# Attention and top-1 MoE in one kernel: more row blocks transposed by DMA, a filled row ring, more output buffers

## The chip, the cores and the metric

One core of one Trainium2 chip. The metric is the device time of one execution in microseconds, the median of several runs. TensorE (PE, with its weight loads PEld), VectorE (DVE), ScalarE (ACT), GpSimd (POOL) and SyncE (SP) each run their own instructions in order. SP issues most DMAs, POOL the indirect ones (gathers and scatters of rows).

## The reference

A causal attention over a window of 64 positions (8 batches, 8 heads, 576 positions, 64 wide), and behind it a mixture of 8 experts of which each token takes one:

```python
scores = scale * np.matmul(q, k.transpose(0, 1, 3, 2))
mask = (rel >= 0) & (rel < 64)               # rel = query position - key position
attn = softmax(np.where(mask, scores, -1e9))
x = np.matmul(attn, v)                       # as 4608 rows of 512
logits = x @ w_gate                          # 8 experts
e = argmax(logits); gate_w = softmax(logits)[e]
out = gate_w * (relu(x @ w1[e]) @ w2[e])     # w1 512 x 1024, w2 1024 x 512
```

All of it is float32. The kernel splits each operand of the expert matmuls into a high and a low part (names ending in h and l, or hi and lo) and adds three products.

## The kernel before

**Attention.** A loop over 36 tiles of 128 rows (variable i, to 42 because each tile goes through stages) makes scores, exponentials, transposes, values and rows, writes each tile of rows to `xs` in DRAM, and computes its routing. q, k and v come through a ring in SBUF, which is given back after the loop (`st.close()`), so that later pools take its place.

**Early passes.** The routing of the first 16 and 28 tiles gives a fixed list of rows for four experts, e = 0 to 3. Each early pass takes two blocks of 128 rows of one expert: POOL gathers them into `xg`, `turn` (four PE transposes into PSUM, then a copy on ACT and a subtraction on DVE) lays them out by columns, and `expert` runs over 8 slices j of the hidden width. Pass e = 0 starts inside the attention loop (`forward`), the rest follow it in a loop of steps, seven to a slice.

**A slice.** `expert` splits the weights of the next slice (`split_`: ACT makes `whi` from `raw`, L252, DVE makes `wlo`, L249), does eight hidden matmuls with whi (L322) and four with wlo (L326), then `hh` on ACT (L332) and `hl` on DVE (L333). `flush` then does the output matmuls of the slice before (L294), and after the last slice scales each block into a `ys` buffer on ACT (L281), which POOL scatters to `out` (L282). `hw` gives ys three buffers.

**Weights.** A load on SP (L234) brings a piece of 1 MB, two slices; there are three buffers. In an early pass `split_` asks for the piece after next use only when a piece is begun: piece 2 (slices 4 and 5) at the top of slice 1. The first piece of the next pass is asked for after slice 3. Late passes have `far=True`, which asks earlier.

**Plan and late passes.** While the early passes run, `steps` advances once per step: `plan` computes on DVE how the remaining rows are cut into late passes (many small operations), then `parts` makes six large tables (`here` once, `said` five times, 128 x 1152), and `table` (36 matmuls) gives row numbers for the late passes. `get` gathers their rows into `late_rows`, two buffers of four blocks. Since rows beyond the end are not written, POOL clears both buffers by eight memsets (L1002), one per slice step. Late pass 0 (two blocks) is turned by PE (`flip`) in slices 5 and 6 of the last early pass. From late pass 1 on, `chain` lays out the rows of the next pass without PE: `part` copies 16-bit halves to `planes` on DVE (L832) and issues a DMA transpose on SP (L835), `join` puts the halves together on ACT (L839), `lay` makes xh and xl (L847, L848). Eleven late passes are always there; widths run from 256 to 512 rows, four of them with four blocks.

The order on every engine is the order in which the code emits (`manual_schedule`).

Of the kernel before, what the change touches and what calls it, by code (L numbers as in the profile page):

```python
# [129 lines left out]
def window_attention_then_top1_moe(ctx: ExitStack, tc: tile.TileContext, qkv, wall, wg, cst, out):  # L130
# [141 lines left out]
    def flush(final=False):  # L272

        if not late:
            return
        (hh, hl), yp, (hi, lo), j, w, last = late.pop()
        def finish(u):
            n = min(P, w - u * P)
            ix, gate = last[0][u][0:n], last[1][u][0:n]
            ys = hw.tile([P, C], F32, name="ys")  # L280
            nc.scalar.activation(out=ys[0:n], in_=yp[u][0:n], func=AF.Copy, scale=gate)  # L281
            ins = nc.gpsimd.indirect_dma_start(  # L282
                out=out, out_offset=bass.IndirectOffsetOnAxis(ap=ix, axis=0), in_=ys[0:n], in_offset=None,
                bounds_check=N - 1, oob_is_err=False)

            for o in outs:
                tc.declare_no_dep(ins.ins, o.ins, reason="scatters to rows of their own")
            outs.append(ins)

        for u, y in enumerate(yp):  # L290
            n = min(P, w - u * P)
            us = slice(u * P, u * P + n)
            for m, (x, ww) in enumerate(((hh, hi), (hh, lo), (hl, hi))):
                nc.tensor.matmul(y[0:n], lhsT=x[:, us], rhs=ww[:, C:], start=(j == 0 and m == 0),  # L294
                                 stop=(j == NJ - 1 and m == 2))
            if final:
                finish(u)
            if u + 1 < len(yp):
                yield
        if last is not None and not final:  # L300
            for u in range(len(yp)):
                finish(u)
        yield
# [399 lines left out]
    def plan():  # L703
# [93 lines left out]
        keep["want"] = want  # L797
        for b in parts(xn, want[:, 0:NMA], NT, NMA):
            keep["said"] = b
            yield  # L800
            yield

    def table(lo, hi):
        read(gathered(keep["said"], NT, hi - lo, t_b), hi - lo, idx_sb[:, lo:hi], gate_sb[:, lo:hi])
# [22 lines left out]

    halves, joined = {}, {}

    def part(i, u):  # L830
        pl = xq.tile([P, 2, C], U16, name="planes", bufs=3)
        nc.vector.tensor_copy(out=pl, in_=late_rows[i % 2][:, u].bitcast(U16).rearrange("p (f s) -> p s f", s=2))  # L832
        src = pl.rearrange("p s f -> p (s f)")
        halves[i, u] = xq.tile([P, 2 * 4, P], U16, name="halves", bufs=4)
        nc.sync.dma_start_transpose(out=halves[i, u], in_=src)  # L835

    def join(i, u):
        x = joined[i, u] = xq.tile([P, 4, P], F32, name="joined", bufs=3)
        nc.scalar.copy(out=x.rearrange("p k t -> p (k t)").bitcast(U16).rearrange("p (t s) -> p s t", s=2),  # L839
                       in_=halves.pop((i, u)).rearrange("p (s k) t -> p s (k t)", s=2))  # L840

    def lay(i, u):
        if u == 0:
            xt[i] = columns(xw)
        x, us = joined.pop((i, u)), slice(u * P, (u + 1) * P)
        xh, xl = xt[i]
        nc.scalar.copy(out=xh[:, :, us], in_=x)  # L847
        nc.vector.tensor_tensor(out=xl[:, :, us], in0=x, in1=xh[:, :, us], op=ALU.subtract)  # L848

    def open_weights(i):  # L850
        wts[i] = Weights(expert_of(passes[i][0]), far=True)
# [8 lines left out]
    def first_passes():  # L860
        for e in range(EARLY):
            ms = range(2 * e, 2 * e + 2)
            for j in expert(xe[e % 2], cols(eidx, ms), cols(egate, ms), ew[e],
                            lambda: ew[e + 1] if e + 1 < EARLY else wts[0]):
                if e + 1 < EARLY and j == 3:
                    ew[e + 1] = Weights(e + 1)
                if e + 1 < EARLY and j in (4, 5):
                    turn(xg[(e + 1) % 3], j - 4, xe[(e + 1) % 2])
                    if (e, j) == (EARLY - 2, 5):
                        keep["turned"] = True  # L870
                yield e, j

    def do(what):
        if rs_[what]:
            rs_[what], f = None, rs_[what]
            f()
# [18 lines left out]
    with tc.manual_schedule():  # L895
        keep_busy(BUSY[0])
        for i in range(NS + LAST):
            for c in range(FIRST, 2 * NS):

                if c % 2 and i == (c - RING + 1) // 2 + 4:  # L900
                    load(c)
            if i == LOADW:
                ew[0] = Weights(0, len(QUARTERS))
            if i == SPLIT:
                ew[0].prepare(AHEAD, pieces)
            if i == TURN:
                ew[0].first = ew[0].split()

            rs_["step"] = i
            each(exps, i - 1)  # L910
            each(evac, i - 2)
            each(apart, i - 2)
            for _ in range(1 if i < NS else 2):
                if gets and gets[0][0] <= i:
                    gets.popleft()[1]()
            if i == TURN:
                scored[1].close()
                turns["hp"] = single(1)
            while exs:
                exs.popleft()()  # L920
            if i > 5 and settled:
                settled.popleft()()
            if i > TURN:
                split_ahead()
            forward(i, 0)
            do("first")
            each(scores, i)
            each(folded, i)
            each(largest, i)
            if i < len(BUSY) - 1:  # L930
                keep_busy(BUSY[i + 1])
            forward(i, 1)
            each(values, i - 3)
            if slow and slow[0][0]:
                f = slow.popleft()[1]
                if f:
                    f()
            while begin and begin[0][0] <= i:
                begin.popleft()[1]()
            for c in range(FIRST, 2 * NS):  # L940
                if c % 2 == 0 and i == (c - RING) // 2 + 3:
                    load(c)
            if quarters and quarters[0][0] <= i:
                _, o, w = quarters.popleft()
                nc.sync.dma_start(out=o, in_=w)
            if rs_["fast"] and (rs_["fast"][0][0] < i):
                rs_["fast"].popleft()[1]()
            forward(i, 2)
            each(rows_t, i - 4)
            each(cols_t, i - 4)  # L950
            forward(i, 3)
            each(transp, i - 1)
            if i == TURN - 1:
                scored[0].close()
                turns.update(xp=[t_b], yp=single(0))
                for u in range(2):
                    turn(xg[0], u, xe[0], turns["yp"][u])
            do("last")
            each(shares, i - 3)
            do("read")  # L960
            for k in range(RATE[0] if i < NS else 4):
                if slow and not slow[0][0]:
                    slow.popleft()[1]()
            for k in range(RATE[1] if i < NS else 2):
                if puts and not slow:
                    puts.popleft()()
            while lows:
                lows.popleft()()
            if pieces:
                pieces.popleft()()  # L970
# [4 lines left out]
        xw = ctx.enter_context(tc.tile_pool(name="xw", bufs=2))  # L975
        xn = ctx.enter_context(tc.tile_pool(name="xn", bufs=1))
        late_rows = [xn.tile([P, MOST, C], F32, name=f"rows{i}") for i in range(2)]
        clear = deque(t[:, u] for t in late_rows for u in range(MOST))
        xq = ctx.enter_context(tc.tile_pool(name="xq", bufs=2))
        turns["xp"].append(m_b)  # L980
        turns["yp"] = [x_b[:, 0], x_b[:, 1], *turns["yp"]]

# [1 line left out]
        def steps():  # L984
# [3 lines left out]
            for _ in range(WAIT[1]):  # L988
                yield
            table(0, NMA)  # L990
            while "turned" not in keep:
                yield
            get(0)
            yield
            open_weights(0)
            get(1)

        rest = steps()
        for e, j in early:
            next(rest, None)  # L1000
            if clear and j is not None:
                nc.gpsimd.memset(clear.popleft(), 0.0)  # L1002
            if e == EARLY - 1 and j == NJ - 3:
                for _ in rest:
                    pass
            if e == EARLY - 1 and j is not None and j >= NJ - 3:
                flip(0, [j - NJ + 3])

    def chain(first, last):
        for i in range(first, last):  # L1010
# [4 lines left out]
            for j in expert(xt.pop(i), cols(idx_sb, passes[i]), cols(gate_sb, passes[i]), wts.pop(i), fol, widths[i]):  # L1015
                if j is None or i + 1 == last:
                    continue
                if j == 2 and i + 2 < last:
                    get(i + 2)
                if j == 3:  # L1020
                    open_weights(i + 1)
                if j in (4, 6):
                    wts[i + 1].load()
                for u, at in enumerate(JOIN[len(passes[i + 1])]):
                    if j == u // 2:
                        part(i + 1, u)
                    if j == at:
                        join(i + 1, u)
                for u, at in enumerate(JOIN[len(passes[i + 1])]):
                    if j == at + 1:  # L1030
                        lay(i + 1, u)
        for _ in flush(True):
            pass

# [50 lines left out]
```

## Time and profile before

| | |
|---|---|
| three runs, us | 627.82, 628.63 (median), 630.64 |
| profiled execution, own time and span, us | 627.76, 626.0 |
| PE busy | 589.2 (94%) |
| DVE busy | 382.0 (61%) |
| ACT busy | 351.5 (56%) |
| POOL busy | 198.9 (32%) |
| granted TensorE clock, mean | 0.996 of full |
| DMA | 129.17 MB, 206 GB/s on average |

Busy time is that of the engine's own instructions, and the span runs from the first to the last instruction. The rows further below give engine, line, operation, output and inputs by the program's names and, in brackets, idle time before the instruction and what ended it.

### The profile page before, as it was taken

The page shows a single profiled execution, that of the slowest core. Times are in us where ns is not written, and L with a number is a line of the kernel's source. Part 1 is how long each engine was busy: PE and PEld are TensorE (multiplying, and loading weights), DVE is VectorE, ACT ScalarE, POOL GpSimd, SP SyncE. Part 2 cuts the span into 40 slices and gives each one's busy share as a digit, 9 for nine tenths or more (in the row PEclk, how much of TensorE's full clock was granted, in tenths as well). Part 3 has the DMA queues.
Part 4 walks back from the last instruction along what each step waited for, and adds up shares of the span by engine and source line. Part 5 has one row for each costly group of instructions (what it writes and reads, how often), then busy time and mean ns, then how long its engine had stood idle before and what let it go on. Part 6 is the DMA issues. An engine that isn't in the chain of part 4 may idle for free. (4 is left out here: it accounts for less than half of the span.)

```text
span 626.0 us, 15826 instructions
## 1 busy us (share of the span) xinstructions
PE 589.2 (94%) x6491; PEld 504.7 (81%) x6491; DVE 382.0 (61%) x692; ACT 351.5 (56%) x729; POOL 198.9 (32%) x188
## 2 busy tenths in 40 slices
PE   8789988898988999999999999999999899999994
PEld 4678877787777799988888888878878799999983
DVE  3677778996789956658554444345244346667651
ACT  4677766776444536476745446356245445657651
POOL 3656667578242141044040050130220312132011
PEclk9999999999999999999999999999999999999998
DMA  9978888954545476397858275396283454886731
GB/s 311 360 250 293 290 262 287 305 195 159 203 173 177 141 279 238 136 302 186 276 143 289 68 169 222 90 148 256 70 229 130 122 208 109 293 283 189 265 113 36
DMA packets 64387, 129.17 MB, mean 206 GB/s; under 512 B 36268, under 2 KB 37420, under 8 KB 56880
## 3 DMA queue, kind: packets, MB, share of 16 engines
q1 hardware_dynamic: 58000, 109.17, 54.3%
q0 software_dynamic: 6304, 18.88, 9.7%
q8 instruction: 53, 0.87, 0.6%
q14 instruction: 30, 0.25, 0.1%
HBM read 102.34 MB, written 19.53 MB: 195 GB/s over the span
## 5 line engine op out<-in xcount | busy, mean ns | idle before, releaser
L249 DVE TENSOR_TENSOR wlo<-raw,whi 128x1024 fp32r<-128x1024 f32 (+1 forms) x126 | 149.1, 1184 | 77.9 <-ACT whi L252 77.7
L332 ACT ACTIVATE hh<-e_b 128x256 fp32r<-128x256 f32 (+4 forms) x120 | 53.5, 446 | 172.2 <-PE e_b L326 172.0
L282 POOL DMA_INDIRECT out<-ys,idx_sb x32 | 37.0, 1157 | 273.8 <-ACT ys L281 269.2
L252 ACT CAST whi<-raw 128x1024 fp32r<-128x1024 f32 (+1 forms) x121 | 121.4, 1004 | 1.8 <-DMA raw<-wall 1.7
L322 PE MATMUL e_b<-xh,whi 128*128 128x256 f32 (+4 forms) x352 | 109.7, 328 | 3.2 <-ACT whi L252 3.2
L333 DVE SCALAR_TENSOR_TENSOR hl<-e_b,hh 128x256 fp32r<-128x256 f32 (+4 forms) x120 | 59.6, 497 | 85.9 <-ACT hh L332 85.6
L322 PE MATMUL e_b<-xl,whi 128*128 128x256 f32 (+4 forms) x352 | 108.8, 325 | 0.0
L459 POOL TENSOR_TENSOR pm<-tsb,cs 128x512 f32<-128x512 f32 x72 | 90.4, 1277 | 50.5 <-ACT tsb L452 43.1
L322 PEld LDWEIGHTS e_b<-xh,whi 128*128 128x128 f32 x352 | 66.2, 188 | 13.1 <-ACT whi L252 5.4
L326 PE MATMUL e_b<-xh,wlo 128*128 128x256 f32 (+4 forms) x352 | 72.0, 327 | 0.0
L322 PEld LDWEIGHTS e_b<-xl,whi 128*128 128x128 f32 x352 | 66.2, 188 | 6.2
L443 ACT ACTIVATE pf<-s_b,mxs 128x64 f32<-128x64 f32 x288 | 63.1, 339 | 10.5 <-DVE mxs L435 8.6
L473 PE MATMUL x_b<-ring,pm 64*64 64x65 f32 x2176 | 47.8, 222 | 15.4 <-issue 6.5
L326 PEld LDWEIGHTS e_b<-xh,wlo 128*128 128x128 f32 x352 | 56.7, 188 | 4.2 <-DVE wlo L249 0.2
L473 PEld LDWEIGHTS x_b<-ring,pm 64*64 64x64 f32 x2176 | 42.0, 134 | 21.2 <-issue 13.3
L294 PE MATMUL e_b<-whi,hl 128*128 128x512 f32 x144 | 56.4, 392 | 1.0 <-DVE hl L333 1.0
L294 PE MATMUL e_b<-whi,hh 128*128 128x512 f32 x144 | 56.8, 395 | 0.0
L294 PE MATMUL e_b<-wlo,hh 128*128 128x512 f32 x144 | 56.5, 393 | 0.0
L497 ACT COPY xT<-m_b 128x512 f32<-128x512 f32 x36 | 21.1, 587 | 40.9 <-PE m_b L490 40.9
L190 POOL DMA_INDIRECT rows<-xs,idx_sb x32 | 38.4, 1200 | 13.9 <-issue 12.7
L416 PE MATMUL s_b<-ring 64*64 64x128 f32 x1024 | 41.0, 278 | 0.0
L839 ACT COPY joined<-halves 128x1024 uint16<-128x1024 uint16 x30 | 39.9, 1350 | 0.0
(193 smaller groups left out, 1021.3 us busy)
## 6 DMA issues: line engine op xcount, KB each, us to landing
raw<-wall SPq DMA_DIRECT2D x58, 1024.0 KB, 6.1
ring<-qkv SPq DMA_DIRECT2D x66, 386.0 KB, 5.0
xs<-xrow SPq DMA_DIRECT2D x36, 256.0 KB, 3.4
raw<-wall SPq DMA_DIRECT2D x8, 256.0 KB, 5.5
ring<-qkv SPq DMA_DIRECT2D x4, 256.0 KB, 4.6
ring<-qkv SPq DMA_DIRECT2D x4, 130.0 KB, 4.7
ring<-qkv SPq DMA_DIRECT2D x1, 512.0 KB, 3.7
rows<-xs,idx_sb POOLq DMA_INDIRECT x32, 6.4
```

The lines of the kernel that those rows point to most:

```text
L249: nc.vector.tensor_tensor(out=lo[:, s], in0=raw[:, s], in1=hi[:, s], op=ALU.subtract)
L252: nc.scalar.copy(out=hi[:, s], in_=raw[:, s])
L294: nc.tensor.matmul(y[0:n], lhsT=x[:, us], rhs=ww[:, C:], start=(j == 0 and m == 0), stop=(j == NJ - 1 and m == 2))
L322: nc.tensor.matmul(hp[:, 0:w], lhsT=hi[:, ks], rhs=x[:, kk, 0:w], start=(kk == 0 and x is xh), stop=False)
L326: nc.tensor.matmul(hp[:, 0:w], lhsT=lo[:, kk * P:(kk + 1) * P], rhs=xh[:, kk, 0:w], start=False, stop=(kk == 3))
L332: nc.scalar.activation(out=hh[:, 0:w], in_=hp[:, 0:w], func=AF.Relu)
L333: nc.vector.scalar_tensor_tensor(out=hl[:, 0:w], in0=hp[:, 0:w], scalar=0.0, in1=hh[:, 0:w], op0=ALU.max, op1=ALU.subtract)
L416: nc.tensor.matmul(sp[cols, a, g], lhsT=q_r[rows, r, g], rhs=k_r[rows, r - 1:r + 1, g], start=True, stop=True)
L443: nc.scalar.activation(out=pf[:, g, a], in_=sp[:, a, g, 0], func=AF.Exp, bias=mx[:, h:h + 1], scale=SCALE)
L459: nc.gpsimd.tensor_tensor(out=pm[i], in0=t.rearrange("p (g q) -> p g q", g=NG), op=ALU.mult, in1=cc("mask")[:, i * P:(i + 1) * P].unsqueez ...
L473: nc.tensor.matmul(x_b[cols, a, g * V1:(g + 1) * V1], lhsT=pm[i][rows, g, cols], rhs=v_r[rows, c % RING - i, g], start=(i == 0), stop=(i = ...
L839: nc.scalar.copy(out=x.rearrange("p k t -> p (k t)").bitcast(U16).rearrange("p (t s) -> p s t", s=2), in_=halves.pop((i, u)).rearrange("p ...
```

## The change

- `part`, `join` and `lay` take rows and a key instead of a pass, and `prepare` calls them for any pass. Early passes e = 2 and e = 3 are prepared that way during the pass before (slices 0, 4, 5 and 6), and late pass 0 during e = 3 by `ready`. Pass e = 1 is still turned by PE.
- `ready` also holds what `chain` did at slices 3, 4 and 6: it opens the next late pass's weights and loads two pieces. For late pass 0 this now happens in e = 3.
- `get(0)` no longer waits for the last `turn`; `rest` is run to its end after e = 2.
- The late rows are filled by two loads of 1 MB from `xs` on SP instead of by eight memsets on POOL.
- `ys` has five buffers.
- The six parts of the late table are twice as many steps apart, so that the table comes 24 steps later.
- In the last turn of the attention loop the delayed low halves (`lows`) are emitted before the routing work, not after it.

```diff
-            ys = hw.tile([P, C], F32, name="ys")
+            ys = hw.tile([P, C], F32, name="ys", bufs=5)
...
             keep["said"] = b
-            yield
-            yield
+            for _ in range(4):
+                yield
...
+    def part(rows, key):
+        pl = keep["xq"].tile([P, 2, C], U16, name="planes", bufs=3)
+        nc.vector.tensor_copy(out=pl, in_=rows.bitcast(U16).rearrange("p (f s) -> p s f", s=2))
+        halves[key] = keep["xq"].tile([P, 2 * 4, P], U16, name="halves", bufs=4)
+        nc.sync.dma_start_transpose(out=halves[key], in_=pl.rearrange("p s f -> p (s f)"))
...
+    def prepare(j, rows, nu, key, xt):
+        for u in range(nu):
+            at = JOIN[nu][u]
+            if j == u // 2:
+                part(rows[:, u], (key, u))
+            if j == at:
+                join((key, u))
+        for u in range(nu):
+            if j == JOIN[nu][u] + 1:
+                lay((key, u), u, xt())
+
+    def ready(i, j):
...
+        prepare(j, late_rows[i % 2], len(passes[i]), i, columns_of)
+        if j == 3:
+            open_weights(i)
+        if j in (4, 6):
+            wts[i].load()
...
-                if e + 1 < EARLY and j in (4, 5):
-                    turn(xg[(e + 1) % 3], j - 4, xe[(e + 1) % 2])
-                    if (e, j) == (EARLY - 2, 5):
-                        keep["turned"] = True
+                if e == 0 and j in (4, 5):
+                    turn(xg[1], j - 4, xe[1])
+                if 0 < e < EARLY - 1 and j is not None:
+                    prepare(j, xg[(e + 1) % 3], 2, ("early", e), lambda: xe[(e + 1) % 2])
+                if e == EARLY - 1 and j is not None:
+                    ready(0, j)
...
+            if i == NS + LAST - 1:
+                while lows:
+                    lows.popleft()()
...
-        clear = deque(t[:, u] for t in late_rows for u in range(MOST))
-        xq = ctx.enter_context(tc.tile_pool(name="xq", bufs=2))
+        for t in late_rows:
+            nc.sync.dma_start(out=t, in_=xs[0:MOST * P].rearrange("(u p) c -> p u c", p=P))
+        keep["xq"] = ctx.enter_context(tc.tile_pool(name="xq", bufs=2))
...
             table(0, NMA)
-            while "turned" not in keep:
-                yield
             get(0)
             yield
-            open_weights(0)
             get(1)
...
-            if clear and j is not None:
-                nc.gpsimd.memset(clear.popleft(), 0.0)
-            if e == EARLY - 1 and j == NJ - 3:
+            if (e, j) == (EARLY - 2, NJ - 1):
                 for _ in rest:
                     pass
-            if e == EARLY - 1 and j is not None and j >= NJ - 3:
-                flip(0, [j - NJ + 3])
...
-                if j == 3:
-                    open_weights(i + 1)
-                if j in (4, 6):
-                    wts[i + 1].load()
...
+                ready(i + 1, j)
```

## Rows read from the trace of the kernel before

**Rows 1.** Stretches: length, busy time of each engine, granted clock, DMA share, GB/s.

```profile
core 0: us, PE busy (x) PEld busy (x) DVE busy (x) ACT busy (x) POOL busy (x), PEclk, DMA share, GB/s
...
190.00:200.00 10.00, 7.92 (x51) 6.65 (x50) 9.44 (x32) 2.97 (x6) 2.33 (x5) 1.00 0.67 238
210.00:220.00 10.00, 9.09 (x55) 7.40 (x54) 10.00 (x12) 5.13 (x8) 3.19 (x2) 1.00 0.48 158
...
540.00:550.00 10.00, 10.00 (x67) 9.09 (x66) 7.11 (x9) 7.31 (x11) 0.00 (x0) 1.00 0.66 249
```

**Rows 2.** Waits of PE, 176 to 218: total us, times, longest.

```profile
PE e_b L326 <- DVE wlo L249: 2.3, 4, 1.3
PE x_b L294 <- DVE hl L333: 2.0, 2, 1.6
PE e_b L294 <- DVE hl L333: 1.0, 1, 1.0
PE m_b L793 <- DVE xel L204: 0.5, 1, 0.5
```

**Rows 3.** Waits of PE, 355 to 505.

```profile
PE e_b L322 <- ACT whi L252: 3.0, 4, 1.8
```

**Rows 4.** Waits of ACT, 355 to 505.

```profile
ACT ys L281 <- DMA out<-ys,idx_sb: 16.5, 4, 4.3
```

**Rows 5.** Timeline of PE at a turn: start, us, instruction.

```profile
229.66 0.60 PE L201 MATMUL m_b<-cs,xg 128*128 128x128 f32 x4
230.02 0.36 PE L322 MATMUL e_b<-xeh,whi 128*128 128x256 f32 x1
```

**Rows 6.** Timeline of DVE in a late pass of 256.

```profile
550.46 1.28 DVE L832 COPY planes<-rows 128x1024 uint16<-128x1024 uint16 x2
```

**Rows 7.** Timeline of ACT in late pass 0.

```profile
278.72 1.05 ACT L252 CAST whi<-raw 128x1024 fp32r<-128x1024 f32 x1 [1.21 <-DMA raw<-wall]
...
279.94 1.35 ACT L839 COPY joined<-halves 128x1024 uint16<-128x1024 uint16 x1
```

**Rows 8.** Timeline of POOL, the memsets.

```profile
181.13 1.47 POOL L1002 MEMSET rows<- 128x512 f32 x3
...
189.92 2.41 POOL L1002 MEMSET rows<- 128x512 f32 x5
```

**Rows 9.** Timeline of DVE, three small operations of the plan.

```profile
180.38 2.25 DVE L681 TENSOR_SCALAR nbr<-nb 128x8 f32<-128x8 f32 x1
...
183.08 0.16 DVE L681 TENSOR_SCALAR half<-left 128x8 f32<-128x8 f32 x1
...
190.82 1.54 DVE L679 TENSOR_SCALAR l<-l 128x8 f32<-128x8 f32 x1
```

**Rows 10.** Line 234, loads at 196.18 (early), 554.07 and 530.68 (behind transposes).

```profile
DMA to landing us min/median/max: 4.8/4.8/4.8
...
DMA to landing us min/median/max: 6.8/6.8/6.8
...
DMA to landing us min/median/max: 8.1/8.1/8.1
```

**Rows 11.** Timeline of PE, first matmuls of slices 0 and 1 of e = 1.

```profile
184.25 0.28 PE L322 MATMUL e_b<-xeh,whi 128*128 128x256 f32 x1
...
187.06 0.28 PE L322 MATMUL e_b<-xeh,whi 128*128 128x256 f32 x1
```

**Rows 12.** Timeline of PE, the table of the late passes.

```profile
220.79 2.67 PE L640 MATMUL t_b<-said,hot_row 128*128 128x160 bf16 x36
```

**Rows 13.** Timeline of POOL, the first gather of late rows.

```profile
224.69 1.44 POOL L190 DMA_INDIRECT rows<-xs,idx_sb  x1 [4.45 <-issue]
```

**Rows 14.** Line 190, the five gathers of late rows from 224.69 to 230.7.

```profile
DMA to landing us min/median/max: 3.8/5.3/6.7
```

**Rows 15.** Timeline of PE, first matmul of a late pass of 256.

```profile
548.06 0.28 PE L322 MATMUL e_b<-xh,whi 128*128 128x256 f32 x1
```

**Rows 16.** Timeline of SP in the same pass.

```profile
551.17 2.64 SPq L835 DMA_TRANSPOSE halves<-planes  x2
554.07 1.22 SPq L234 DMA_DIRECT2D raw<-wall  x1
```

More of the change, by code (lines that the diff above doesn't have):

```diff
@@ L828, in window_attention_then_top1_moe @@
     halves, joined = {}, {}
[L830 to L838, printed above, removed]
-        nc.scalar.copy(out=x.rearrange("p k t -> p (k t)").bitcast(U16).rearrange("p (t s) -> p s t", s=2),
-                       in_=halves.pop((i, u)).rearrange("p (s k) t -> p s (k t)", s=2))
@@ L842, in lay @@
[L842 to L846, printed above, removed]
+    def part(rows, key):
[3 more added lines that the diff above has]
+        nc.sync.dma_start_transpose(out=halves[key], in_=pl.rearrange("p s f -> p (s f)"))
@@ L847, in lay, with join @@
+    def join(key):
+        x = joined[key] = keep["xq"].tile([P, 4, P], F32, name="joined", bufs=3)
+        nc.scalar.copy(out=x.rearrange("p k t -> p (k t)").bitcast(U16).rearrange("p (t s) -> p s t", s=2),
+                       in_=halves.pop(key).rearrange("p (s k) t -> p s (k t)", s=2))
+    def lay(key, u, xt):
+        x, us = joined.pop(key), slice(u * P, (u + 1) * P)
+        xh, xl = xt
         nc.scalar.copy(out=xh[:, :, us], in_=x)
         nc.vector.tensor_tensor(out=xl[:, :, us], in0=x, in1=xh[:, :, us], op=ALU.subtract)
+    def prepare(j, rows, nu, key, xt):
[8 more added lines that the diff above has]
+                lay((key, u), u, xt())
@@ L850, in open_weights, with columns_of @@
+    def ready(i, j):
+        def columns_of():
+            if i not in xt:
+                xt[i] = columns(xw)
+            return xt[i]
+        prepare(j, late_rows[i % 2], len(passes[i]), i, columns_of)
[3 more added lines that the diff above has]
+            wts[i].load()
     def open_weights(i):
@@ L1019, in chain @@
                     get(i + 2)
-                if j == 3:
-                    open_weights(i + 1)
-                if j in (4, 6):
-                    wts[i + 1].load()
[L1024 to L1031, printed above, removed]
+                ready(i + 1, j)
         for _ in flush(True):
```

## The prediction

> **What bounds the kernel now.** I read a table of stretches first, then what PE waited for, then what ScalarE waited for. In the late passes PE has no gap (10.00 of 10 us in 540 to 550), but in the early ones it has (7.92 and 9.09) while VectorE is at 9.4 to 10 tenths [rows 1]. From 176 to 218 PE waits for VectorE 8 times, 5.8 us in all: for low halves of weights (wlo) and of hidden values (hl), and once for an xel [rows 2]. From 355 to 505 it waits 4 times for whi, 3.0 us [rows 3], and ScalarE, which makes whi, waits as often for a scatter that still reads a ys buffer, 16.5 us [rows 4]. The reader is to see that time can come from these 8.8 us, or from work taken off PE, and from nothing else that the change touches.
>
> Durations come from the profiled execution: span 626.0, its own time 627.76, so 1.76 around. The median shown is 628.63, 0.87 above it. A measurement of this kernel can tell about 0.5% (3.1 us) from no change.
>
> **Part 1, transposes off PE.** Six blocks (two each of early passes e = 2 and e = 3 and of late pass 0) lose their four PE transposes. Such a four begins at 229.66, the next matmul at 230.02 [rows 5]: 6 x 0.36 = 2.1 us less. In their place come, per block, a planes copy on DVE (1.28 for two [rows 6]), a DMA transpose and a joined copy on ACT (1.35 [rows 7]); the copy and the subtraction behind them stay. ACT's 6 x 1.35 = 8.1 us are hidden: it is busy 3.0 and 5.1 tenths in the early rows, and in 540 to 550 the same chain runs at 7.3 tenths beside a PE at 10.00 [rows 1]. If ACT had no room they would cost up to 8. The Trainium skill (TensorE: Matmul & The Clock Gate, Part 4: PE-mode transpose) gives about 275 ns for one transpose in a kernel; by it 24 would be 6.6 us, and the sum 4.5 lower. That a four takes 0.36 shows that they overlap; I keep the row.
>
> **Part 2, five ys buffers.** A late pass of four blocks scales four ys in a row, and the fourth waits for the first one's scatter. There are four such passes and four waits [rows 4]. With five buffers none of four waits, and whi, which stands behind it on ACT, is in time. Bounds 0 (another wait takes its place) to 3.0; value 2.9, as nothing else delays ACT there.
>
> **Part 3, memsets off POOL.** While POOL fills the late rows (three memsets from 181.13 on, five from 189.92 [rows 8]), two DVE operations on 8 columns take 2.25 and 1.54, where one of their kind takes 0.16 [rows 9]; both end as the memsets end (182.6 and 192.3). Without memsets DVE gets back 2.09 + 1.38 = 3.5 us. In the second early pass (e = 1) it gets two planes copies for it, 1.3. DVE has hardly a gap there and PE waits for it, so what DVE is spared reaches the end: 2.2. Bounds: 0 (copies beside small operations cost more) to 3.5.
>
> The fill from DRAM instead is two loads of 1 MB on SP's queue. One weight load of that size lands in 4.8 us by itself [rows 10], so at most 9.6 for both. They are emitted in the first early pass, ahead of the second weight piece (two slices each) of e = 1. That piece is first needed for slice 2, two slices of 2.81 after 184.25 [rows 11], at 189.9. The memsets of the same tiles, emitted at the same place, began at 181.13 [rows 8]. I take an earlier start and 0, since SP has little else to wait for. If the fill began as late as 181, the piece would land at 181 + 9.6 + 4.8 = 195.5 and PE lose 195.5 + 1.1 - 189.9 = 6.7; that end goes into the range.
>
> **Part 4, table parts twice as far apart, lows earlier.** Some parts leave the stretch around 210 where DVE is at 10.00, but the two planes copies for e = 3 come there. Without the three longest waits (1.3, 1.6 and 1.0) 1.9 us of [rows 2] remain; bounds -1.9 to +1.5 (copies on a full DVE), value 0, as what goes and what comes are alike. The lows flushed earlier put a wlo ahead of routing work. Its wait, the 1.3, goes, but the hl queued behind is then late by nearly as much: 0.3 less (0 to 1.3).
>
> The table moves from slice 2 to slice 6 of e = 2 (24 steps, 7 a slice). Its matmuls start at 220.79 and take 2.67 [rows 12], the gather goes out at 224.69 [rows 13] and lands 3.8 to 6.7 later [rows 14]: 7.7 to 10.6 after the table starts. The planes copy that now waits for it stands at the end of slice 0 of e = 3: 2.7 of table, some 5.2 of slices 6 and 7, and 2.4 of slice 0 later, 10.3. Queued behind it on DVE are wlo and hl, which PE needs some 2 us later. So 0, at worst 1 to 2 (the second block is gathered later).
>
> **Part 5, the wait that the change adds.** SP issues in order. In e = 1, 2 and 3 two DMA transposes now stand on SP and wait for the planes copies of slice 0. Behind them stands the weight piece for slices 4 and 5, asked for at the top of slice 1 (these weights are not "far": one piece ahead). Before, SP could ask for it as soon as a buffer was free. In a late pass of the same width slice 0 begins at 548.06 [rows 15], the planes copies at 550.46 [rows 6], the transposes go out from 551.17 and the next load at 554.07 [rows 16]: 6.0 after the slice. It lands L later. Then whi takes 1.1 (1.05 in the wait of this kind that late pass 0 has at 278.72 [rows 7]). Slice 4 begins 4 x 2.81 = 11.25 after slice 0 [rows 11]. So each pass stalls 6.0 + L + 1.1 - 11.25 = L - 4.15. Where DVE is late at slice 0 (e = 1 and 2), both sides shift about alike. L is 4.8 for a load alone, 6.8 and 8.1 behind such transposes [rows 10] in late passes, whose code gathers rows at the same time. The early ones don't, so I take 5.5, nearer to the first: 1.35 a pass, 4.0 in three. In late passes the same order costs nothing, as that piece is for slice 6.
>
> **Sum.** -2.1 - 2.9 - 2.2 + 0 - 0.3 + 4.0 = -3.5: 624.3 on the profiled execution's basis, 625.1 on that of the median. I predict 624.5.
>
> **Rivals.**
> - The weight piece is not late (L at or below 4.15, or SP reaches it earlier). For it: loads without transposes in front land in 4.8, and PE waited for no load in 176 to 218 [rows 2]. Against: the order of issue in [rows 16]. Then the 4.0 fall away: 627.8 - 7.5 = 620.3.
> - Slower: the piece lands as late as behind the late transposes, L = 8.1. Each pass stalls 3.95, 11.9 in all, and the sum is +4.4: 632. It decides from L = 6.65 (sum zero) and is 0.5% slower from 7.7. For it: both landings measured behind transposes. Against: the gathers beside those. The Trainium skill (DMA: Bandwidth & Descriptors, Queues, rings and completion order) says that descriptors are taken in ring order on each DMA engine, so the load's bytes would follow the transposes'; the longer landings of [rows 10] agree.
> - DVE and ACT gain nothing: copies and parts keep DVE as far behind as before (part 3 gives 0), and the ys waits turn into another wait (part 2 gives 0). For it: DVE stays near full. Against: the stretched operations of [rows 9] and the four equal counts of [rows 3, 4]. Sum -2.1 - 0.3 + 4.0 = +1.6: 629.4, no change.
>
> **How the numbers follow.** Forecast 0.55, its own range 621.5 to 627.5 (L from 4.8 to 6.2, part 3 from 1 to 3); piece not late 0.23; slower 0.12; nothing gained 0.10. The range 619.5 to 629.5 takes in the forecast, the first rival and the last, and leaves out the slower one and a sum of all the good bounds. Faster by over 0.5% is below 625.5: 0.22 from the second case and 0.35 from the forecast, 0.57. Slower by over 0.5%: most of the slower rival, 0.10. Within: 0.33.
>
> **What would show it.** Right: no transposes of rows on PE after 200; the two DVE operations at 0.16; no wait of ACT for a scatter and none of PE for whi in 355 to 505; and a new PE wait for whi, released by a raw load, at slice 4 of e = 1, 2 and 3, one to two us each, with that load right behind two transposes on SP. Wrong: that wait absent (then 620) or 3 to 4 us (then 630 or more); a DVE wait for gathered rows at slice 0 of e = 3; or a wait for weights at slice 2 of e = 1, which would be the fill's.

## The result and the profile after

The changed kernel took 636.88 us (median of 4 runs, 636.50 to 639.66) beside 629.63 for the kernel before in the same comparison: ratio 1.0124, interval 1.0080 to 1.0169. It is slower; 624.5 was forecast, with 629.5 as the upper end. The profiled execution took 636.73 us, span 634.9, mean granted clock 0.985 (before: 627.76, 626.0, 0.996). Two executions of the versions below (630.94 and 1994.15 us) ran in a slow state and count in no median or ratio.

The wait that part 5 forecast is there, three times and longer each time. Timeline of PE after the change: start, duration, line, instruction, in brackets the idle time before it and what ended it.

```profile
198.53 0.39 PE L322 MATMUL e_b<-xeh,whi 128*128 128x256 f32 x1 [1.93 <-ACT whi L252]
228.51 0.58 PE L322 MATMUL e_b<-xeh,whi 128*128 128x256 f32 x1 [4.38 <-ACT whi L252]
260.93 0.39 PE L322 MATMUL e_b<-xeh,whi 128*128 128x256 f32 x1 [4.62 <-ACT whi L252]
292.81 0.39 PE L322 MATMUL e_b<-xh,whi 128*128 128x256 f32 x1 [1.74 <-ACT whi L252]
```

The first three are slice 4 of e = 1, 2 and 3, 10.9 us in all; the fourth stands at slice 6 of late pass 0, where nothing was forecast. The second one is followed back here. SP in e = 2 (two transposes, the piece for slices 4 and 5, then two further pieces), and how long each of these three loads took to land:

```profile
216.52 2.65 SPq L834 DMA_TRANSPOSE halves<-planes  x2
219.28 1.42 SPq L234 DMA_DIRECT2D raw<-wall  x1
220.81 0.87 SPq L234 DMA_DIRECT2D raw<-wall  x2
```

```profile
DMA to landing us min/median/max: 8.1/8.1/8.1
...
DMA to landing us min/median/max: 9.1/9.1/9.1
...
DMA to landing us min/median/max: 11.3/11.3/11.3
```

The piece asked for at 219.28 lands 8.1 later, at 227.4, and there ACT's idle time ends:

```profile
227.41 1.04 ACT L252 CAST whi<-raw 128x1024 fp32r<-128x1024 f32 x1 [7.72 <-DMA raw<-wall]
```

Behind the stall the clock is low. Stretches of 2 us (length, busy time of PE, PEld, DVE, ACT, POOL, granted clock, DMA share, GB/s):

```profile
224.00:226.00 2.00, 0.14 (x1) 0.00 (x0) 0.00 (x0) 0.00 (x0) 0.00 (x0) 1.00 0.95 379
226.00:228.00 2.00, 0.00 (x0) 0.00 (x0) 0.00 (x0) 0.59 (x1) 0.00 (x0) 0.78 0.99 418
228.00:230.00 2.00, 1.49 (x7) 1.49 (x8) 1.51 (x2) 1.68 (x3) 0.00 (x0) 0.50 0.95 393
230.00:232.00 2.00, 2.00 (x9) 1.90 (x9) 2.00 (x3) 0.52 (x2) 0.00 (x0) 0.50 0.16 66
232.00:234.00 2.00, 2.00 (x7) 1.52 (x5) 0.79 (x2) 1.99 (x2) 0.00 (x0) 0.51 0.47 82
234.00:236.00 2.00, 2.00 (x16) 1.87 (x15) 1.31 (x2) 0.50 (x2) 0.00 (x0) 1.00 0.79 315
```

PE stands still for some four microseconds while the DMA engines are full, and works at the 1.2 GHz level (0.50) until 234: 7 to 9 matmuls in 2 us, and 16 once the clock is back. In stretches of 10 us the clock is 0.84 (200 to 210), 0.86, 0.80 (220 to 240) and 0.83 (260 to 270), at least 0.99 elsewhere: (0.16 + 0.14 + 0.20 + 0.17) x 10 = 6.7 us, some 0.7 of it while PE stood still (from about 227.1 to 228.5).

The gains came as well. PE's waits from 176 to 218, which answer to [rows 2], are these:

```profile
PE e_b L326 <- DVE wlo L249: 2.4, 3, 1.3
PE e_b L322 <- ACT whi L252: 1.9, 1, 1.9
PE x_b L294 <- DVE hl L333: 0.2, 1, 0.2
```

VectorE's share fell from 5.8 to 2.6 us. The small operation that had taken 1.54 [rows 9] is short again:

```profile
190.46 0.17 DVE L679 TENSOR_SCALAR l<-l 128x8 f32<-128x8 f32 x1
```

The other one, of 2.25, takes 0.17 as well, at 180.49.

From 355 to 505 PE waits for nothing and ACT for no scatter ([rows 3, 4]: 3.0 and 16.5). The fill went out at 165.69, landed in 11.4 us (at most 9.6 was forecast), and nothing waited for it.

The cost lies in one stretch. ACT scales the results of a pass at its end (ys), so these lines date the end of the first early pass and of late pass 0. Before and after:

```profile
186.57 1.38 ACT L281 ACTIVATE ys<-e_b,egate 128x512 f32<-128x512 f32 x2 [0.31 <-PE e_b L294]
...
288.65 1.39 ACT L281 ACTIVATE ys<-e_b,gate_sb 128x512 f32<-128x512 f32 x2 [0.26 <-PE e_b L294]
```

```profile
185.40 1.38 ACT L281 ACTIVATE ys<-e_b,egate 128x512 f32<-128x512 f32 x2 [0.31 <-PE e_b L294]
...
301.63 1.38 ACT L281 ACTIVATE ys<-e_b,gate_sb 128x512 f32<-128x512 f32 x2 [0.26 <-PE e_b L294]
```

102.1 us became 116.2, which is 14.1 more; the rest of the span is 5.2 shorter. Between these lines PE is busy for 98.4 us before and for 101.8 after, so it stands idle for 3.7 and 14.5: 3.4 and 10.8 more make the 14.1. Of the idle time after, 12.7 are the four waits for whi. The busy time grows by the low clock while PE works (6.7 - 0.7 = 6.0) and shrinks by the transposes (2.1 by [rows 5]), which would give 3.9. Below, "the stretch" is this one.

### The profile page after: what moved, and what is told of

Its sections match the earlier page's. It is cut to its first block, busy times and chain, and to the rows that moved or that the text cites. A ratio compares the mean times of both kernels' runs of the same rounds, so it can differ in the third digit from the quotient of the medians.

```text
span 634.9 us, 15798 instructions
## 1 busy us (share of the span) xinstructions
PE 590.9 (93%) x6467; PEld 507.1 (80%) x6467; DVE 382.6 (60%) x698; ACT 358.7 (56%) x735; POOL 195.2 (31%) x180
## 4 chain that ended last, share of the span: by engine, by line
PE 68%; issue 10%; DVE 7%; DMA 7%; POOL 4%; ACT 3%; SPq 1%; POOLq 0%; DVEq 0%; ACTq 0%
PE e_b L322 18%; PE e_b L294 11%; PE e_b L326 9%; DMA raw<-wall 7%; PE x_b L294 6%; PE t_b L294 5%; PE x_b L473 4%; PE m_b L294 4%; PE s_b L416 3%; POOL pm L459 3%; PE m_b L490 2%; PE m_b L534 1%; ACT whi L252 1%; PE t_b L448 1%; DVE wlo L249 1%
## 5 line engine op out<-in xcount | busy, mean ns | idle before, releaser
L252 ACT CAST whi<-raw 128x1024 fp32r<-128x1024 f32 (+1 forms) x121 | 121.5, 1005 | 26.5 <-DMA raw<-wall 26.5
L282 POOL DMA_INDIRECT out<-ys,idx_sb x32 | 39.4, 1231 | 272.6 <-ACT ys L281 267.1
L322 PE MATMUL e_b<-xh,whi 128*128 128x256 f32 (+4 forms) x352 | 109.4, 327 | 2.3 <-ACT whi L252 2.3
L322 PE MATMUL e_b<-xl,whi 128*128 128x256 f32 (+4 forms) x352 | 108.8, 325 | 0.0
L322 PEld LDWEIGHTS e_b<-xh,whi 128*128 128x128 f32 x352 | 66.3, 188 | 11.1 <-ACT whi L252 3.3
L322 PEld LDWEIGHTS e_b<-xl,whi 128*128 128x128 f32 x352 | 66.2, 188 | 6.4
L443 ACT ACTIVATE pf<-s_b,mxs 128x64 f32<-128x64 f32 x288 | 63.1, 339 | 10.8 <-DVE mxs L435 7.6
L473 PEld LDWEIGHTS x_b<-ring,pm 64*64 64x64 f32 x2176 | 41.6, 134 | 21.3 <-issue 14.5
L838 ACT COPY joined<-halves 128x1024 uint16<-128x1024 uint16 x36 | 48.0, 1350 | 0.0
L190 POOL DMA_INDIRECT rows<-xs,idx_sb x32 | 36.4, 1137 | 31.2 <-PE e_b L326 21.7
L322 PE MATMUL e_b<-xeh,whi 128*128 128x256 f32 x128 | 34.4, 298 | 10.9 <-ACT whi L252 10.9
## 6 DMA issues: line engine op xcount, KB each, us to landing
rows<-xs SPq DMA_DIRECT2D x2, 1024.0 KB, 11.4
```

What stands on the lines that cost most here:

```text
L252: nc.scalar.copy(out=hi[:, s], in_=raw[:, s])
L282: ins = nc.gpsimd.indirect_dma_start(out=out, out_offset=bass.IndirectOffsetOnAxis(ap=ix, axis=0), in_=ys[0:n], in_offset=None, bounds_che ...
L322: nc.tensor.matmul(hp[:, 0:w], lhsT=hi[:, ks], rhs=x[:, kk, 0:w], start=(kk == 0 and x is xh), stop=False)
L443: nc.scalar.activation(out=pf[:, g, a], in_=sp[:, a, g, 0], func=AF.Exp, bias=mx[:, h:h + 1], scale=SCALE)
L473: nc.tensor.matmul(x_b[cols, a, g * V1:(g + 1) * V1], lhsT=pm[i][rows, g, cols], rhs=v_r[rows, c % RING - i, g], start=(i == 0), stop=(i = ...
```

## The experiments

The theory: pieces of weights stand on SP behind two transposes, and are sent together when these are out. The first rival: the transposes' own traffic slows every load near them, wherever they stand. Ratios are to the kernel before on the same chip, with 95% intervals.

**Transposes one slice later** (of the changed kernel, in e = 1 to 3):

```diff
-            if j == u // 2:
+            if j == u // 2 + off:        # off = 1 for early passes and late pass 0
                 part(rows[:, u], (key, u))
```

> The changed kernel with one move: in e = 1, 2 and 3 the planes copies and DMA transposes of the next two blocks are emitted after slice 1 instead of after slice 0, so that on SP the weight piece for slices 4 and 5 stands ahead of them; the number of transposes, copies and loads is the same. Theory 1 (order on SP: the piece is late because it stands behind transposes that wait for DVE, and goes out together with the next two pieces): PE's waits for whi at slice 4 (1.9, 4.4 and 4.6 us) and the clock of 0.5 behind them go, some 15 us in all: 620 to 624. At most a short wait at slice 6, as the next piece now stands behind the transposes. Theory 2 (the transposes' traffic slows the DMA engines wherever it stands): the waits stay, only shifted by a slice: 633 to 638.

624.95 us, 0.9893 (0.9862 to 0.9925). The waits for whi between 180 and 330 fall from 13.3 us to 0.8, and the clock is 1.00 there. SP in e = 2: the piece goes out at 209, ten microseconds earlier than in the change, and the transposes are sent after it.

```profile
209.06 0.33 SPq L234 DMA_DIRECT2D raw<-wall  x1
220.34 2.61 SPq L834 DMA_TRANSPOSE halves<-planes  x2
223.06 1.01 SPq L234 DMA_DIRECT2D raw<-wall  x2
```

```profile
PE e_b L326 <- DVE wlo L249: 3.2, 3, 1.7
PE e_b L322 <- ACT whi L252: 0.8, 2, 0.5
```

The traffic is the same and the loss is gone, so the order on SP is what cost it. (The third line shows that two pieces still go out together behind the transposes; they are for later slices.)

**Loads further ahead, transposes where the change puts them:**

```diff
-                    ew[e + 1] = Weights(e + 1)
+                    ew[e + 1] = Weights(e + 1, far=True)
+                if e + 1 < EARLY and j in (4, 6):
+                    ew[e + 1].load()
```

> The changed kernel with the weights of e = 1, 2 and 3 asked for as those of late passes are (far: one piece after slices 3, 4 and 6 of the pass before, the fourth at slice 2). The transposes stay where they are. Theory 1 (order on SP): three of four pieces are there before the transposes, the fourth is needed only at slice 6: no wait for whi in e = 1 to 3, 617 to 622, of which 15 to 17 us come from the waits and the clock. Theory 2 (traffic of the transposes): loads that share the DMA engines with transposes land in 8 to 9 us still, but none is needed so soon, so this run alone doesn't tell the theories apart; it says what the order of requests is worth.

622.48 us, 0.9852 (0.9794 to 0.9911). One wait for whi of 0.8 us is left between 180 and 330. So the change is faster than the kernel before once its loads are ahead of the transposes.

**Two parts alone on the kernel before**: five ys buffers; and the fills from DRAM in place of the memsets (both edits as in the change).

> The kernel before with five ys buffers and nothing else. Forecast of the prediction's part 2: the four waits of ACT for a scatter go and with them 3.0 us of PE's waits for whi: ratio 0.995, 626 to 627. Rival (another wait takes their place): ratio 1.000.

629.0 us, 0.9946 (0.9914 to 0.9977). No wait of PE after 285 is left. 0.54% of 632 is 3.4 us.

> The kernel before with the late rows filled by two loads from DRAM instead of eight memsets on POOL, and nothing else. Forecast of part 3: the two DVE operations on 8 columns take 0.16 each, and 2.5 to 3.5 us of PE's waits for hl and wlo between 180 and 218 go: ratio 0.995, 626 to 627. Rival: DVE stays near full there and the waits come back a slice or two later, under 1 us gained, ratio 0.998 to 1.000. If the fill delayed the weight piece behind it, PE would wait for whi in e = 1: ratio above 1.000.

628.09 us, 0.9946 (0.9915 to 0.9977), again 3.4. The waits for hl that [rows 2] had at 2.0 and 1.0 are down to 0.4. PE's waits from 170 to 285:

```profile
PE e_b L326 <- DVE wlo L249: 2.3, 4, 1.3
PE x_b L516 <- DVE egate L648: 0.5, 1, 0.5
PE m_b L793 <- DVE xel L204: 0.5, 1, 0.5
PE e_b L322 <- ACT whi L252: 0.4, 1, 0.4
PE x_b L294 <- DVE hl L333: 0.4, 1, 0.4
```

**All of the change but the transposes.** Built from the kernel before, with parts 2, 3 and 4 and all rows turned by PE.

> The kernel after with all six pairs of transposes back on TensorE: five buffers of scaled rows, the two fills from DRAM, the table's parts spread and the waiting weight halves written out, without part 1. If the parts add up (five buffers alone 0.9946, fills alone 0.9946, spread and halves about nothing), the ratio to the kernel before is 0.989 (0.9865 to 0.992), with no wait for whi of more than 0.8 us and none for ys. What the version with transposes by DMA and far weights (0.9852) has beyond this is then the price of part 1: 2.1 us were forecast, 0.33%. Rival: the two gains are one and the same (the second only shows when the first is there), ratio 0.9945.

622.25 us, 0.9881 (0.9840 to 0.9922). The gains of parts 2 and 3 add up. The stretch takes 100.2 us (186.96 to 287.12), and PE waits for no load in it.

**Transposes by DMA for late pass 0 alone:**

```diff
-                if e == 0 and j in (4, 5):
-                    turn(xg[1], j - 4, xe[1])
-                if 0 < e < EARLY - 1 and j is not None:
-                    prepare(j, xg[(e + 1) % 3], 2, ("early", e), lambda: xe[(e + 1) % 2])
+                if e + 1 < EARLY and j in (4, 5):
+                    turn(xg[(e + 1) % 3], j - 4, xe[(e + 1) % 2])
```

> The kernel after with the rows of the two early passes turned by TensorE again and only those of the first late pass by DMA. Theory: each stall stands for itself; the waits of 1.93 and 4.38 us go with their low clock, the one of about 4.6 us in the last early pass stays with its 2 us of low clock, and so do 1.7 to 2.3 us in the first late pass: ratio 0.989 + (4.6 + 2 + 2 - 0.7)/630 = 1.0015 (0.998 to 1.005). Rival: the third stall is as long only because the two before it put the loads out of step; alone it is 1.4 to 2 us as in the first of the three passes, ratio 0.992 to 0.995.

628.44 us, 0.9967 (0.9937 to 0.9997), between the two. One stall is left in e = 3, with 1.7 us lost to the low clock behind it and 1.1 us of waiting in late pass 0; the piece had landed in 7.2 us, one of three sent within 2.4 us.

```profile
251.16 0.39 PE L322 MATMUL e_b<-xeh,whi 128*128 128x256 f32 x1 [3.44 <-ACT whi L252]
```

So a stall comes without the two before it, but it is 1.2 shorter than the 4.62 that it was behind them, as its piece lands in 7.2 and not in 9.0: theory and rival each hold in part, and the ratio lies between their ranges.

**Is it the loads sent together that make the first one late?** In e = 2 alone, the fourth piece and the next pass's first go out from ScalarE's queue, behind the cast of slice 4:

```diff
+            apart = isinstance(self.ev, int) and self.ev == 2 and (jj, r) == (2, 0)
-            while self.loaded < min(jj + 2, NJ // 2):
+            while self.loaded < min(jj + 2, NJ // 2) and not apart:
...
                 piece(slice(0, 2 * C))
+                if apart:
+                    self.load(nc.scalar)
...
-                    ew[e + 1] = Weights(e + 1)
+                    ew[e + 1] = Weights(e + 1, queue=nc.scalar if e == 2 else None)
```

> The kernel after; in the third early pass alone (the second of the three with DMA transposes) the weight piece behind the two transposes goes out by itself: the fourth piece and the next pass's first one are asked for from ScalarE's queue, the fourth behind the cast of slice 4, the first behind the ReLU of slice 3. Theory (three loads that go out within 2 us share the DMA engines, so the first lands late): that piece lands in 5 to 5.7 us in place of 8.1, the wait at slice 4 there is 0.8 to 1.6 us in place of 4.38, the low clock behind it shrinks, ratio 1.0035 to 1.0085; the stalls of the passes before and after it stay at 1.9 and 4.6. Rival (the transposes' own traffic, or the load by itself, is what takes 8 us): landing 8.1 and wait 4.4 as before, ratio 1.0125.

638.61 us, 1.0123 (1.0081 to 1.0166). The piece, now by itself behind the transposes, lands in 6.6 in place of 8.1, and the wait falls by as much, from 4.38 to 2.82 (L325 and L253 here are L322 and L252):

```profile
DMA to landing us min/median/max: 6.6/6.6/6.6
```

```profile
201.09 0.39 PE L325 MATMUL e_b<-xeh,whi 128*128 128x256 f32 x1 [1.33 <-ACT whi L253]
...
228.96 0.58 PE L325 MATMUL e_b<-xeh,whi 128*128 128x256 f32 x1 [2.82 <-ACT whi L253]
```

Sharing is worth 1.5 of the 3.3 us between 8.1 and a load alone (4.8 [rows 10]), by one trace of each; behind the transposes a load is still 1.8 slower, so theory and rival each hold in part. The clock was low for as long as after the 4.38 (below). Where nothing was edited, the stalls are 1.33 in e = 1 and 5.05 in e = 3, beside 1.93 and 4.62 in the change. The stretch is 2.8 us shorter than in the change (113.4), which the times don't show. Behind the wait of 1.33 the clock did not fall at all.

```profile
204.00:206.00 2.00, 2.00 (x14) 1.69 (x12) 1.90 (x7) 1.66 (x2) 0.00 (x0) 1.00 0.06 25
...
228.00:230.00 2.00, 1.04 (x5) 1.04 (x6) 1.06 (x1) 2.00 (x3) 0.00 (x0) 0.57 0.56 115
230.00:232.00 2.00, 2.00 (x10) 2.00 (x10) 2.00 (x4) 0.20 (x2) 0.00 (x0) 0.50 0.96 406
232.00:234.00 2.00, 2.00 (x6) 1.52 (x6) 1.24 (x2) 2.00 (x3) 0.00 (x0) 0.50 1.04 438
234.00:236.00 2.00, 2.00 (x14) 1.90 (x13) 1.23 (x1) 0.44 (x1) 0.00 (x0) 0.72 0.99 356
```

The 1.8 need not be the transposes' alone. POOL's scatters of the finished pass go out just ahead of the piece (in the change at 218.25 in e = 2 and at 249.12 and 250.45 in e = 3, before loads at 219.28 and 250.86), and in e = 3 its gathers for the late passes too (241.06 to 247.43). What POOL's queue (q0) moved in the changed kernel while the piece of e = 2, then that of e = 3, was on its way (packets, MB, share of the 16 DMA engines):

```profile
q0 software_dynamic: 146, 0.35, 15.6%
...
q0 software_dynamic: 203, 0.57, 26.3%
```

In e = 1 it moved nothing meanwhile, in the change as in this run, and there the first of three loads behind two transposes landed in 5.7 and 5.0. The version with all rows turned by PE shows the other side: no transpose by DMA goes out there before late pass 0, yet loads sent at 187.4 and 239.0, alone on SP for the next 5 us, landed in 6.9 and 8.1, while POOL's queue took 19.3 and 43.7%. So POOL's traffic alone can cost as much as the 1.8. No run takes it away beside the transposes, and how the 1.8 divides stays open.

**Far weights, and the transposes for the first two late passes one slice later** (`off` = 1 for passes 0 and 1).

> The version with far early weights (0.9852) and the transposes of the second late pass's rows given out one slice later. Theory: the one wait for whi left there (0.8 us at 277) came from a load behind two transposes whose planes came late; it goes, ratio 0.984. Rival: that stretch is bound by the DMA engines (share 1.04 to 1.09 from 264 to 276), so the wait only moves or ScalarE waits for the turned rows instead: 0.985 to 0.988.

623.66 us, 0.9888 (0.9853 to 0.9923). The wait did not go (1.4 at one place, 0.8 before), and ACT now waits for the turned rows:

```profile
272.79 1.36 ACT L838 COPY joined<-halves 128x1024 uint16<-128x1024 uint16 x1 [1.58 <-DMA halves<-planes]
```

So the rival's account holds: the loads gain nothing there, and the turned rows come late as well.

**What part 1 and part 4 are worth without the stalls.** Far early weights throughout; once with part 1 and without part 4, once with neither, and the same without far weights:

> Transposes by DMA, five buffers, fills from DRAM, far early weights; the table's parts and the waiting halves as in the kernel before. Beside the run below that has the transposes on TensorE it gives the price of part 1 without its stalls. As forecast in part 1: 2.1 us less than that run, a ratio to the kernel before lower by 0.0033, near 0.985. Rival: the TensorE time that the transposes give up is taken by other waits, and the two runs lie within 0.001 of each other. If part 4 is worth 0.3 us, as forecast, this run is 0.0005 above the version with part 4 (0.9852 earlier).

> The kernel before with five buffers, fills from DRAM and far early weights; all transposes of the early and the first late pass on TensorE. If far weights matter only behind DMA transposes: the same as the next run, ratio 0.988 to 0.989. Rival: far weights gain by themselves, and part of the 0.9852 was theirs: 0.985.

> The kernel before with five buffers and fills from DRAM alone. The two gains add: 0.9946 times 0.9946, ratio 0.989. If part 4 is worth nothing: equal to the version with it (0.9881) within 0.001; if the spread table matters: 0.990 or more.

0.9927 (0.9901 to 0.9953), 0.9854 (0.9828 to 0.9881) and 0.9875 (0.9849 to 0.9901); medians 627.71, 623.69 and 624.85 us. Far weights gain nothing by themselves that can be told. Without the spread table the transposes by DMA lose, and here the times do show it (0.9927 against 0.9854): the stretch takes 102.0 us (187.93 to 289.97) in place of 98.4 in the version with it, and of 100.5 with PE's transposes. The traces hold only a part of the loss: the two profiled executions are 0.8 us apart (624.85 and 624.07), the medians 4.0. VectorE shows one delay in e = 2. First with the table's parts close together, then apart:

```profile
213.09 1.35 DVE L632 TENSOR_TENSOR said<-here,val 128x1152 bf16<-128x1152 bf16 x1
214.69 1.35 DVE L632 TENSOR_TENSOR said<-here,val 128x1152 bf16<-128x1152 bf16 x1
215.95 1.22 DVE L249 TENSOR_TENSOR wlo<-raw,whi 128x1024 fp32r<-128x1024 f32 x1
217.42 1.35 DVE L632 TENSOR_TENSOR said<-here,val 128x1152 bf16<-128x1152 bf16 x1
218.69 1.29 DVE L832 COPY planes<-xg 128x1024 uint16<-128x1024 uint16 x2
```

```profile
212.25 1.35 DVE L632 TENSOR_TENSOR said<-here,val 128x1152 bf16<-128x1152 bf16 x1
213.52 1.22 DVE L249 TENSOR_TENSOR wlo<-raw,whi 128x1024 fp32r<-128x1024 f32 x1
214.99 1.29 DVE L832 COPY planes<-xg 128x1024 uint16<-128x1024 uint16 x2
```

Close together, the planes copies come 3.7 us later, and so do the transposes and the loads behind them.

**The waiting low half two steps earlier** than in the kernel before, on top of parts 2 and 3:

```diff
             if i > TURN:
                 split_ahead()
+            if i == NS + LAST - 2:
+                while lows:
+                    lows.popleft()()
```

> The run above with the waiting weight half written two steps before the end of the routing loop, right behind the split, so that VectorE does it in its idle time at 173 and not behind the two hot_row products. Theory: the change's own edit of this kind moved no instruction past another; this one takes away the wait of 1.34 us for wlo at 178 to 181 in every kernel so far, 1.3 us, ratio lower than that of the run above by 0.002. Rival: the routing chain that it is put ahead of comes out 1.2 us later and TensorE waits there instead: no difference.

624.19 us, 0.9860 (0.9832 to 0.9888). The wait of 1.3 for wlo near 180 is gone (2.3 us in 4 waits between 176 and 330 became 1.0 in 3); in the time, 0.9860 and 0.9875 can't be told apart.

**Part 1 alone, everything else equal:** far weights, spread table and the earlier half, with the rows turned by DMA, then by PE.

> The whole change with far early weights, and the waiting half written two steps earlier in place of the change's own edit of it. Against the next run, which differs in the six pairs of transposes alone: if these are worth the 2.1 us forecast for part 1 once the loads are not held up, this one is lower in ratio by 0.0033, at about 0.983, and the stretch from the end of the first early pass to the end of the first late pass is about 2 us shorter (98 to 99 us against 100 to 101). Rival: the copies that split and join the rows (0.64 us each on VectorE, 1.35 on ScalarE) bring waits for the weights' low halves that eat the 2.1 us, and both stand within 0.001.

> Five buffers, fills from DRAM, the table's parts spread, far early weights and the waiting half written two steps earlier; all transposes of the early and the first late pass on TensorE. 0.986 by the runs before it (0.9881 without far weights and the earlier half, 0.986 with the half alone). Rival for part 1: equal to the run above within 0.001.

623.06 us, 0.9880 (0.9833 to 0.9927), and 622.85 us, 0.9865 (0.9818 to 0.9912): no difference that the times can show. In the traces the stretch takes 98.8 us with DMA transposes and 102.4 with PE's:

```profile
187.06 1.38 ACT L281 ACTIVATE ys<-e_b,egate 128x512 f32<-128x512 f32 x2 [0.31 <-PE e_b L294]
...
285.90 1.39 ACT L281 ACTIVATE ys<-e_b,gate_sb 128x512 f32<-128x512 f32 x2 [0.26 <-PE e_b L294]
```

```profile
188.49 1.38 ACT L281 ACTIVATE ys<-e_b,egate 128x512 f32<-128x512 f32 x2 [0.31 <-PE e_b L294]
...
290.87 1.39 ACT L281 ACTIVATE ys<-e_b,gate_sb 128x512 f32<-128x512 f32 x2 [0.26 <-PE e_b L294]
```

Paired also with the earlier two (98.4 with far weights and DMA, 100.2 with PE), the traces give 1.4 to 4.0 us for part 1, one trace each; 0.9 of it is a wait for a load that only the version of 102.4 has (0.94 at 251.83). Whether any of this reaches the time stays open. Eight versions between 0.985 and 0.989 beat both kernels, and the times do not rank them. The version with parts 2 and 3 alone (0.9875) is one of them, so no time on record shows that parts 1 and 4 add to it.

## Why the prediction was wrong

**The step that failed is part 5**, "each pass stalls L - 4.15" with L taken as 5.5 and a sum of +4.0. Its mechanism holds, and its formula within 0.5 us; the term L was mis-sized (5.7, 8.1 and 9.0 measured), and a second term behind it was missing.

- The formula: pieces that landed in 5.7, 6.6, 7.2, 8.1 and 9.0 us should stall PE by 1.6, 2.5, 3.1, 4.0 and 4.9; measured were 1.93, 2.82, 3.44, 4.38 and 4.62.
- L: the prediction set 4.8 for a load alone against 6.8 and 8.1 behind late transposes [rows 10], put the difference down to gathers, held that the early passes have none, and went near the first. In e = 1 this fits: POOL's queue moves nothing, and L is 5.7. In e = 2 and 3 the premise fails: POOL's scatters, in e = 3 also the gathers that part 4 had moved there, take 15.6 and 26.3% of the DMA engines while the piece is on its way, and L is 8.1 and 9.0 (behind the late transposes of [rows 10] POOL's share was 27.6 and 29.4%). Besides, while SP waits for the planes, buffers for the next pieces come free as well, and all go out within 2 to 3 us; the run with the piece by itself shows 1.5 us for that. The measured sum is 10.9 us of stall in place of 4.0; how the rest of L divides between transposes and POOL stays open.
- The price of a stall: the prediction counted idle time alone. The low clock behind it adds up to 6.7 us. The rival "slower" had L = 8.1 and 632; with the clock on top it is near the measured case. It had 0.12, and both rows behind transposes spoke for it.
- Late pass 0, forecast at nothing ("that piece is for slice 6"), got a wait of 1.74 at slice 6. The order there is the same before the change, where PE waited 0.22 at this slice: it had no slack to lose, and the piece landed in 8.8 us in place of 7.3.

**The other steps.** Part 2: -2.9 forecast, 3.4 by the run of its own, the waits gone as said. Part 3: -2.2 forecast with 1.3 of planes copies taken off; the run of its own has no such copies, and its 3.4 answers to the 3.5. The fill cost nothing. Part 1: -2.1 forecast, 1.4 to 4.0 in the stretch, not resolved in the time. The Trainium skill's 275 ns for one transpose (TensorE: Matmul & The Clock Gate, Part 4: PE-mode transpose) would make it 6.6, an estimate; the traces are nearer to the row of 0.36 for four. Part 4: the table's parts were set at 0 with a bound of -1.9; undoing part 4 beside DMA transposes makes the stretch 3.7 longer, so the bound was too narrow. Beside PE transposes the stretches differ by 0.7 (100.9 and 100.2). Its lows: -0.3 forecast, nothing in fact. The wait of 1.34 is still there at 178.28, since the edit moved no instruction of VectorE past another. And the first rival's condition, that the piece is not late, is what the two mended versions bring about: their ratios of 0.9893 and 0.9852 would make 621 and 618 of the 627.8 that the prediction started from, beside the 620.3 of that rival.

What ScalarE's copies cost was forecast as hidden. PE's waits for ScalarE in the two mended versions are short (0.8 us for whi in each, and 0.5 for hh in the first), and no run tells how much of them is the copies'.

## What to carry to other kernels

Before putting an instruction that waits onto a queue which also issues prefetches, list what stands behind it on that queue, when each was asked for before, and how many of them will then go out at once: the first of a burst is the one that is needed. Price the landing by a row from behind the same kind of neighbour, with the other queues' traffic at that time, and a stall of PE by its idle time plus the low clock that can follow it. Two parts that look harmless each (tables on a full VectorE, copies that a queue waits for) are tried together, since one decides how late the other is.

## What the runs showed of the hardware

The granted clock does not follow the length of a stall in proportion: behind 1.33 and 1.74 us it stayed at 1.00, behind 1.93 it fell to 0.50 for about 3 us, behind 3.44 and 4.62 for about as long, and behind 2.82 and 4.38 it was low for 5 to 6 us after the work began again. Shortening a stall from 4.38 to 2.82 gave back idle time but no clock.

A load of 1 MB landed in 4.8 us alone, 6.6 by itself behind two transposes and beside POOL's scatters, 5.0 to 9.3 as the first of three behind transposes, 11.3 as a last one. As the first of three it took 5.0 and 5.7 where POOL's queue moved nothing, and 6.8 to 9.3 where that queue took 15 to 38% of the DMA engines' time. With no transpose near and 43.7% it took 8.1. The Trainium skill (DMA: Bandwidth & Descriptors, Queues, rings and completion order) has descriptors taken in ring order on each DMA engine; the longer landing behind the transposes agrees with it, but that the first of three is slower than one alone does not follow from that order by itself.
